# Four moves in the SP queue and half-size sums in the last unit of an attention and MLP kernel

## The chip, the cores and the metric

The program runs on one core of one Trainium2 chip. The time is the device time of one execution in microseconds (us). Before the change it is 294.99 us, the median of three runs (294.71 to 295.28).

## The reference

The inputs are q, k, v of 4 batches, 8 heads, 768 positions and 64 numbers each, a projection of 64 x 6, a gain of 512, and two weight matrices (512 x 2048 and 2048 x 512). Cut to what matters:

```python
q_bits = (q @ proj) > 0                          # six bits for each query, and for each key
k_bits = (k @ proj) > 0
mask   = (q_bucket[:, :, :, None] == k_bucket[:, :, None, :])   # all six bits agree
scores = np.where(mask, q @ k.T / 8, -1e9)
attn   = softmax(scores)
x      = (attn @ v), heads side by side          # 4 x 768 x 512
xn     = (x - mean) / sqrt(var + 1e-6) * g_ln    # over the 512
out    = x + np.maximum(xn @ w_ch1, 0) @ w_ch2
```

## The kernel before

**Work.** The 3072 rows of the output are cut into 12 units of 256 rows; unit u belongs to batch u // 3. A unit has two parts. In its attention, for each of two groups g of four heads and three pairs of key blocks (step s = 6u + 3g + kp), `S` multiplies bits and queries with keys into the PSUM tile `sc` (L570), `E` takes the exponential on ScalarE (L576), and `A` multiplies with v into `acc` (L595). `na` and `nb` divide by the row sums into the tile `x`, `nc` and `ag` make mean and variance, `rs` the inverse root on GpSimd (L635), and `ce` writes the centred rows `xc` in bf16 (L630), 128 rows at a time. In its MLP, `fl` turns `xc` into `xnT` with a DMA transpose, one for each 128 rows (L639). `F.u.p` is block p (256 of the 2048 hidden numbers) of the first layer (L659, eight matmuls), which needs both halves of `xnT`; `R.u.p` is its ReLU into `hb` (L667 on ScalarE, L669 on VectorE). The second layer of units 1 to 11 is a product of 2 x 2 blocks with seven products in place of eight: `P.u.k` is product k (L725, eight matmuls). Its left sides are quarters of `hb`, or the sums S1 to S4 of quarters that `ss.u.k` makes on VectorE (L710); S3 is written over a quarter of `hb`. `Y.u.k` adds what the product's PSUM tile holds to a quarter of `x` (L730). `O` stores finished rows (L742 and L744).

**PSUM.** The tiles of the tag `f` (first layer, products, bits) take two buffers in turns, by a list of digits in the kernel. Products 1, 6 and 7 add up in one tile X, products 5 and 3 in another, Yb, and in the last unit Ya (product 2), Yb and Yc (product 4) take the same buffer. So each `Y` has to read a tile before the next product adds to it or overwrites it.

**Loads.** `LX` loads 768 KB of q or k (L508), which `tu` turns on VectorE into `T` (L304) and `CA` casts. `hm` multiplies with the projection (L526), `bt` makes bits of it in the tile B, `mw` writes B to DRAM (L544), and four `mr` read it back, spread over the partitions, into G (L547, 24 KB each); `S` of that batch and group waits for all four. `lv` loads v (L467).

**Order.** All of it stands in one list of words, `ORDER`, written out as op.engine.arguments and issued one after the other; the engine letter is t (TensorE), v (VectorE), a (ScalarE), p (GpSimd) or s (the SP queue, which issues most DMAs). Each engine and the SP queue work through their own words in that order, so an instruction that waits holds up what stands behind it on its queue. The semaphores between the queues follow from the tiles that the instructions read and write.

Of the kernel before, what the change touches and what calls it, by code (L numbers as in the profile page):

```python
# [46 lines left out]
S.t.19.2 F.t.1.6 E.a.18.0 rs.p.2 F.t.1.3 CA.p.1.1.1 E.a.19.0 S.t.21.2 O.s.0.0 lv.s.1.4.1  # L47
E.a.19.1 A.t.19.2 E.a.21.0 R.v.1.6 sw.v.3.0 sw.v.2.0 E.a.21.1 F.t.1.0 R.a.1.0 lv.s.2.0.3
R.v.1.3 ce.v.2.1 sw.v.4.0 lv.s.1.4.0 ce.v.2.0 F.t.1.5 A.t.20.2 S.t.22.2 fl.s.2.1 tu.v.2.0.0.2
F.t.1.4 R.a.1.5 cv.p.1.4.0 A.t.18.2 LX.s.2.0.1 E.a.22.0 R.v.1.4 F.t.1.2 sp.t.1.0 sc.v.1.0  # L50
na.v.3.0 E.a.22.1 S.t.23.2 F.t.1.7 R.a.1.2 R.v.1.7 E.a.23.1 cv.v.1.4.2 E.a.23.0 F.t.1.1
sw.v.1.0 fl.s.2.0 R.a.1.1 nb.v.3.0 S.t.24.2 E.a.24.0 E.a.24.1 on.p.2 P.t.1.2 Y.v.1.2
F.t.2.1 R.a.2.1 su.p.1.4 S.t.26.2 lv.s.2.4.0 O.s.0.1 O.s.0.3 A.t.23.2 ss.v.1.1 P.t.1.1
P.t.1.5 ss.v.1.3 ss.v.1.2 tu.v.2.0.1.2 E.a.26.1 E.a.26.0 Y.v.1.1 lv.s.2.0.1 P.t.1.6 A.t.22.2
S.t.25.2 tu.v.2.0.0.3 ss.v.1.4 lv.s.2.4.3 E.a.25.0 Y.v.1.5 tu.v.2.0.0.0 Y.v.1.6 P.t.1.3 Y.v.1.3
# [13 lines left out]
F.t.3.7 R.a.3.7 F.t.3.0 tu.v.2.1.1.0 E.a.33.0 S.t.37.2 E.a.37.1 tu.v.2.1.1.1 E.a.37.0 tu.v.2.1.0.0  # L69
tu.v.2.1.1.3 tu.v.2.1.1.2 hm.t.2.1 O.s.2.0 CA.v.2.1.0 LX.s.3.0.0 bt.v.2.1 mw.s.2.1 mr.s.2.1.1 mr.s.2.1.3  # L70
S.t.38.2 F.t.3.5 R.v.3.0 A.t.34.2 R.a.3.5 F.t.3.3 CA.v.2.1.1 R.a.3.3 tu.v.3.0.1.0 E.a.38.1
A.t.35.2 F.t.3.4 A.t.33.2 O.s.2.2 nb.v.5.0 F.t.3.1 mr.s.2.1.2 R.a.3.4 na.v.5.1 tu.v.3.0.0.3
F.t.3.2 lv.s.3.4.1 E.a.38.0 R.a.3.1 rs.p.4 ce.v.4.1 S.t.36.2 P.t.3.2 R.a.3.2 E.a.36.1
nb.v.5.1 su.p.2.4 ss.v.3.1 Y.v.3.2 P.t.3.1 E.a.36.0 mr.s.2.1.0 S.t.39.2 E.a.39.1 E.a.39.0
O.s.2.3 ce.v.4.0 Y.v.3.1 nc.v.5.0 A.t.37.2 P.t.3.5 ss.v.3.2 ss.v.3.4 fl.s.4.1 LX.s.3.1.0
A.t.36.2 Y.v.3.5 cv.v.2.4.0 P.t.3.6 Y.v.3.6 P.t.3.3 A.t.38.2 ss.v.3.3 S.t.40.2 Y.v.3.3
E.a.40.0 E.a.40.1 P.t.3.7 nc.v.5.1 Y.v.3.7 tu.v.3.0.0.1 fl.s.4.0 F.t.4.3 ag.v.5.0 R.v.4.3
P.t.3.4 Y.v.3.4 O.s.3.1 O.s.3.0 S.t.41.2 E.a.41.1 E.a.41.0 sp.t.2.0 sc.v.2.0 F.t.4.0
ag.v.5.1 rs.p.5 F.t.4.4 R.a.4.4 na.v.6.0 R.v.4.0 O.s.3.3 ce.v.5.1 fl.s.5.1 S.t.44.2
E.a.44.1 tu.v.3.0.1.3 F.t.4.5 A.t.41.2 F.t.4.6 A.t.40.2 tu.v.3.0.0.2 E.a.44.0 R.a.4.6 tu.v.3.0.1.2  # L80
# [42 lines left out]
O.s.8.3 F.t.9.6 R.a.9.6 nb.v.11.0 ss.v.9.1 ss.v.9.2 S.t.70.2 E.a.70.1 A.t.71.2 ss.v.9.3  # L123
O.s.8.2 A.t.69.2 P.t.9.2 Y.v.9.2 ss.v.9.4 P.t.9.1 fl.s.10.0 E.a.70.0 Y.v.9.1 A.t.70.2
na.v.11.1 nb.v.11.1 fl.s.10.1 F.t.10.7 P.t.9.6 R.a.10.7 Y.v.9.6 nc.v.11.0 P.t.9.5 P.t.9.7
Y.v.9.5 Y.v.9.7 nc.v.11.1 P.t.9.3 Y.v.9.3 P.t.9.4 Y.v.9.4 O.s.9.3 O.s.9.0 O.s.9.2
F.t.10.6 R.a.10.6 ag.v.11.1 F.t.10.1 O.s.9.1 ag.v.11.0 rs.p.11 ce.v.11.0 fl.s.11.0 F.t.10.0
R.a.10.1 R.a.10.0 F.t.10.5 R.a.10.5 F.t.10.4 F.t.10.3 R.a.10.4 R.a.10.3 ce.v.11.1 fl.s.11.1
F.t.10.2 R.a.10.2 P.t.10.2 Y.v.10.2 F.t.11.4 R.a.11.4 ss.v.10.1 ss.v.10.2 P.t.10.1 Y.v.10.1
ss.v.10.4 P.t.10.5 Y.v.10.5 P.t.10.6 P.t.10.3 ss.v.10.3 Y.v.10.6 P.t.10.7 Y.v.10.3 F.t.11.0  # L130
R.a.11.0 Y.v.10.7 P.t.10.4 Y.v.10.4 O.s.10.2 F.t.11.2 R.a.11.2 F.t.11.5 R.a.11.5 F.t.11.7
F.t.11.1 R.a.11.7 R.a.11.1 F.t.11.6 F.t.11.3 R.a.11.6 P.t.11.2 R.a.11.3 ss.v.11.1 P.t.11.1
Y.v.11.2 ss.v.11.2 Y.v.11.1 ss.v.11.4 P.t.11.5 P.t.11.6 O.s.10.0 Y.v.11.5 P.t.11.3 ss.v.11.3
Y.v.11.6 P.t.11.7 O.s.10.1 Y.v.11.3 Y.v.11.7 O.s.10.3 O.a.11.0.1 O.s.11.0.0 Y.v.11.7.1.0 O.s.11.1.0.1
O.a.11.1.1.1 P.t.11.4 Y.v.11.4 O.a.11.1.1.0 O.s.11.1.0.0
"""


# [3 lines left out]
    E="012302132023132032103230103231032031230120302123031230120321013202120320",  # L142
# [10 lines left out]
    rs="012102102102",  # L153
# [12 lines left out]
def kernel(  # L166
# [15 lines left out]
    nc = tc.nc  # L182
    P = 128
    B, H, S, D = q.shape
# [11 lines left out]
    A = 4 * (D + 1)  # L196
# [34 lines left out]
    def sb(name, shape, dt, tag, bufs):  # L231
        if name not in made:
            if tag in SLOTS:
                n = taken.get(tag, 0)
                taken[tag] = n + 1
                tag, bufs = f"{tag}_{SLOTS[tag][n]}", 1
            made[name] = pool.tile(shape, dt, name=name, tag=tag, bufs=bufs)
        return made[name]
# [442 lines left out]
    def Hq(u, t, kh):  # L681
        return hb(u)[:, 8 * kh : 8 * kh + 8, P * t : P * t + P]
# [4 lines left out]
    def Ss(u, k):  # L687
        return Hq(u, 1, 0) if k == 3 else sb(f"S{u}{k}", [P, 8, P], BF16, "tp", 3)
# [9 lines left out]
        }[k]  # L698
        eng.tensor_tensor(out, in0, in1, op=op)

    def ss(eng, u, k):
        out, in0, in1, op = {
            1: (1, Hq(u, 1, 0), Hq(u, 1, 1), AOP.add),
            2: (2, None, Hq(u, 0, 0), AOP.subtract),
            3: (3, Hq(u, 0, 0), Hq(u, 1, 0), AOP.subtract),
            4: (4, Hq(u, 0, 1), None, AOP.subtract),
        }[k]
        in0 = Ss(u, 1) if in0 is None else in0
        in1 = Ss(u, 2) if in1 is None else in1
        eng.tensor_tensor(Ss(u, out), in0, in1, op=op)  # L710

    def prod(u, k):
        if k in (1, 6, 7) or (k == 4 and u < NU - 1):
# [21 lines left out]
    def O_(eng, u, *a):  # L735
# [13 lines left out]
        mem=mem, pmem=pmem, tab=tab, lp=lp, sel=sel, pf=pf, p32=p32c, warm=warm, wm=wm, lx=lx, tn=tn, ca=ca, ha=ha, bh=bh, hc=hc, bc=bc, sl=sl, bi=bi, lg=lg, gt=gt, gc=gc,  # L749
        lw1=lw1, wg=wg, lw2=lw2, on=on, lv=lv, cv=cv, su=su, sp=sp, sq=sq, sc=scp, LX=LX, gx=gx, tu=tu, CA=CA, hm=hm, bt=bt, mw=mw, mr=mr,  # L750
        S=S_, E=E_, A=A_, wa=wa, na=na, nb=nb, nc=nc_, ag=ag, ce=ce, rs=rs, fl=fl, ft=ft, fc=fc, F=F_, R=R_, D=D_, Z=Z_, P=P_, Y=Y_, sw=sw, ss=ss, O=O_,
    )
    ENGINES = dict(v=nc.vector, a=nc.scalar, p=nc.gpsimd, s=nc.sync, t=nc.tensor)
# [35 lines left out]
```

## Time and profile before

| | |
|---|---|
| median of three runs | 294.99 us (294.71 to 295.28) |
| profiled execution: its own time | 294.86 us |
| profiled execution: span of the instructions | 293.2 us |
| TensorE (PE) busy | 285.6 us, 97% of the span |
| VectorE (DVE), ScalarE (ACT), GpSimd (POOL) busy | 71%, 70%, 18% |
| TensorE clock granted | full in every slice |
| DMA moved | 34.10 MB, mean 116 GB/s |
| F, eight matmuls of 128x256 (L659) | 273 ns each, 94.2 us in all |
| ss, one sum of 128x1024 bf16 (L710) | 0.68 us |
| Y, one addition of 128x256 f32 (L730) | 0.42 us |
| fl, issue of one DMA transpose on the SP queue (L639) | 1.21 us |

A timeline row gives start, length, engine, line, operation and the number of instructions merged in it. Matmuls overlap: eight matmuls of 256 columns last 1.04 us from the start of the first to the end of the last, and the next eight begin 0.87 us after the first ones when nothing holds them up. The chain of waits goes back from the last instruction and names at each step what released it; its rows give start, length, and what ran.

### The profile page before, as it was taken

The numbers are of one execution on the slowest core, as the hardware profiler recorded it, in microseconds if no ns is written. First come the engines' busy times: TensorE is split into PE (matmuls) and PEld (weight loads), VectorE is DVE, ScalarE is ACT, GpSimd is POOL, SyncE is SP. The second block draws the span as 40 slices with busy tenths as digits, with TensorE's granted clock in tenths as the row PEclk, the third lists the DMA queues.
The fourth block names the chain that finished last, engine by engine and source line by source line (L and its number), as shares of the span: only waits on it lengthen the run. The fifth ranks groups of instructions, "written<-read, shape, count | busy, mean of one in ns | idle before, by whom it ended". The sixth has DMA issues, their size and how long they took to land.

```text
span 293.2 us, 10524 instructions
## 1 busy us (share of the span) xinstructions
PE 285.6 (97%) x4650; PEld 227.7 (78%) x4650; DVE 206.8 (71%) x474; ACT 206.2 (70%) x236; POOL 54.0 (18%) x88
## 2 busy tenths in 40 slices
PE   8999999999999999999999999999999999999994
PEld 4677778648788887878778778877888878897883
DVE  4757899996769795797667995866666654773433
ACT  4689999998966978784865896887793694515240
POOL 5261325222423005000300107210010010000000
PEclk9999999999999999999999999999999999999999
DMA  6999997747744692362330352230410402304022
GB/s 223 302 319 250 216 277 133 139 134 171 174 122 131 134 307 76 127 189 51 98 82 1 83 132 63 60 61 3 92 37 2 74 2 52 78 6 104 2 72 73
DMA packets 31055, 34.10 MB, mean 116 GB/s; under 512 B 15521, under 2 KB 27809, under 8 KB 31010
## 3 DMA queue, kind: packets, MB, share of 16 engines
q1 hardware_dynamic: 25938, 28.72, 35.6%
q0 software_dynamic: 4224, 4.19, 8.9%
q8 instruction: 36, 0.59, 0.9%
q10 hardware_dynamic: 848, 0.53, 0.7%
q14 instruction: 9, 0.07, 0.1%
HBM read 27.86 MB, written 6.88 MB: 118 GB/s over the span
## 4 chain that ended last, share of the span: by engine, by line
PE 91%; DMA 3%; DVE 2%; SPq 1%; ACT 1%; issue 0%; ACTq 0%; DVEq 0%
PE f L659 27%; PE sc L570 18%; PE X L725 13%; PE acc L595 12%; PE Yb L725 7%; PE hp L526 3%; PE Ya L725 3%; PE hf L394 3%; PE f L674 2%; PE warm L363 1%; ACT E L576 1%; DMA G<-Bd 1%; DMA Bd<-B 1%; PE warm L366 1%; DMA xnT<-xc 1%; SPq L547 1%
## 5 line engine op out<-in xcount | busy, mean ns | idle before, releaser
L576 ACT ACTIVATE E<-sc,bias_sb 128x1024 bf16<-128x1024 f32 x144 | 153.1, 1111 | 36.0 <-PE sc L570 32.6
L659 PE MATMUL f<-xnT,w_sb 128*128 128x256 bf16 x768 | 94.2, 273 | 0.7 <-DMA xnT<-xc 0.6
L659 PEld LDWEIGHTS <-w_sb 128*128 128x128 bf16 x768 | 71.4, 98 | 13.6 <-issue 5.7
L667 ACT ACTIVATE hb<-f 128x512 bf16<-128x512 f32 x67 | 39.6, 598 | 34.5 <-PE f L659 34.5
L570 PE MATMUL sc<-qb,kb 32*128 32x256 bf16 x1152 | 52.5, 267 | 0.0
L595 PEld LDWEIGHTS <-E 128*128 128x128 bf16 x1152 | 40.8, 98 | 4.0 <-issue 2.5
L595 PE MATMUL acc<-vaug,E 128*128 128x65 bf16 x1152 | 43.7, 194 | 0.1
L570 PE MATMUL sc<-G 6*128 6x256 bf16 (+1 forms) x576 | 42.7, 273 | 1.1 <-ACT E L576 0.8
L725 PEld LDWEIGHTS <-hb 128*128 128x128 bf16 x352 | 33.4, 98 | 5.4 <-issue 1.3
L570 PEld LDWEIGHTS <-kb 32*128 32x128 bf16 x1152 | 30.5, 93 | 1.5
L635 POOL TENSOR_SCALAR rs<-mv 128x2 f32<-128x2 f32 x12 | 3.3, 277 | 150.4 <-DVE mv L624 150.4
L730 DVE TENSOR_TENSOR x<-X,x 128x256 f32<-128x256 f32 x44 | 18.4, 419 | 16.5 <-PE X L725 16.3
L570 PEld LDWEIGHTS <-G 6*128 6x128 bf16 (+1 forms) x576 | 16.0, 91 | 16.7 <-issue 13.3
L725 PEld LDWEIGHTS <-S 128*128 128x128 bf16 x264 | 25.0, 98 | 4.8 <-issue 1.4
L669 DVE TENSOR_SCALAR hb<-f 128x512 bf16<-128x512 f32 x29 | 19.7, 681 | 12.0 <-PE f L659 11.8
L304 DVE STREAM_TRANSPOSE T<-X 128x384 f32<-128x384 f32 (+2 forms) x52 | 26.1, 535 | 0.0
L725 PE MATMUL Yb<-w_sb,S 128*128 128x256 bf16 x176 | 22.9, 273 | 0.0
L608 DVE SCALAR_TENSOR_TENSOR y<-vsB,acc 128x520 f32<-128x520 f32 x24 | 16.5, 689 | 8.1 <-PE acc L595 7.8
L725 PE MATMUL X<-wt,hb 128*128 128x256 bf16 x168 | 21.8, 273 | 0.0
L617 DVE TENSOR_TENSOR x<-y,rc 128x512 f32<-128x512 f32 x24 | 17.8, 742 | 0.8
L621 DVE BATCH_NORM_STATS2 st<-x 128x6 f32<-128x256 f32 x48 | 17.4, 412 | 0.2
L730 DVE TENSOR_TENSOR x<-Yb,x 128x256 f32<-128x256 f32 x22 | 9.2, 420 | 9.5 <-PE Yb L725 9.5
(95 smaller groups left out, 268.3 us busy)
## 6 DMA issues: line engine op xcount, KB each, us to landing
out_dram<-x SPq DMA_DIRECT2D x45, 128.0 KB
X<-in_k_dram SPq DMA_DIRECT2D x7, 768.0 KB
vn<-in_v_dram SPq DMA_DIRECT2D x24, 192.0 KB
X<-in_q_dram SPq DMA_DIRECT2D x6, 768.0 KB
w_sb<-in_moe_w_ch_dram POOLq DMA_DIRECT2D x8, 512.0 KB, 10.8
vn<-in_v_dram SPq DMA_DIRECT2D x2, 768.0 KB
X<-in_q_dram SPq DMA_DIRECT2D x2, 512.0 KB
Bd<-B SPq DMA_DIRECT2D x6, 96.0 KB
```

The lines of the kernel that those rows point to most:

```text
L304: nc.vector.transpose(d[:, j], s[:, j, kj0 : kj0 + n])
L570: nc.tensor.matmul(sc(s, i // 2)[:, i % 2, 256 * kk : 256 * kk + 256], lh, rh, start=(rep == 0), stop=(rep == 2), skip_group_check=True,)
L576: nc.scalar.activation(E(s)[:, heads(h)], sc(s, h), AF.Exp, scale=EXP_SCALE, bias=bias_sb)
L595: nc.tensor.matmul(acc[:, qt, (D + 1) * i : (D + 1) * (i + 1)], E(s)[:, i, 256 * kk + P * qt : 256 * kk + P * qt + P], vaug(u // 3)[:, 4 * ...
L608: nc.vector.scalar_tensor_tensor(yt(u, g), vs, EPS_ROW, made[f"acc{u}{g}"][:, :, :A], op0=AOP.mult, op1=AOP.add,)
L617: nc.vector.tensor_tensor(xo, a[:, :, :, 0:D], rc.to_broadcast([P, 2, 4, D]), op=AOP.mult)
L621: nc.vector.bn_stats(stats(u)[:, qt, g], xt(u)[:, qt, 256 * g : 256 * g + 256])
L659: nc.tensor.matmul(f1[:, n].rearrange("p (t x) -> p t x", t=2), w1_sb[:, dt, P * nt : P * nt + P], xnT(u)[:, :, dt], start=(dt == 0), stop ...
L667: nc.scalar.activation(hb(u)[:, 2 * p : 2 * p + 2], f1, AF.Relu)
L669: eng.tensor_scalar_max(hb(u)[:, 2 * p : 2 * p + 2], f1, 0.0)
L725: nc.tensor.matmul(f2, lh[:, n], rh[:, n], start=(first and n == 0), stop=(n == 7), skip_group_check=True)
L730: nc.vector.tensor_tensor(x, made[f"{prod(u, k)}{u}"], x, op=AOP.add)
```

## The change

Four groups of words are moved on the SP queue, and the last unit is written otherwise:

1. `LX.s.2.0.1` (768 KB of k) goes behind `fl.s.2.0`; before, it stood between the two transposes of unit 2.
2. The last two reads of bits, `mr.s.2.1.2` and `mr.s.2.1.0`, go ahead of the store `O.s.2.2` and the load `lv.s.3.4.1`, right behind the first two.
3. `LX.s.3.1.0` (768 KB of q) goes behind `fl.s.4.0`; before, it stood between the two transposes of unit 4.
4. The four stores of unit 9 go behind both transposes of unit 11. (Three stores of unit 10 also stand earlier in the list, but in the same place among SP's words.)
5. The first layer of unit 11 takes its blocks in the order 4 0 5 1 7 2 6 3, not 4 0 2 5 7 1 6 3. Each of its four sums is two instructions of 128x512: the first halves of all four stand after `R.a.11.1`, the second halves where the whole sums stood (after the last ReLU, between the Y).

Cut to its core (reflowed lines of the list are left out):

```diff
-F.t.1.4 R.a.1.5 cv.p.1.4.0 A.t.18.2 LX.s.2.0.1 E.a.22.0 R.v.1.4 F.t.1.2 sp.t.1.0 sc.v.1.0
...
-sw.v.1.0 fl.s.2.0 R.a.1.1 nb.v.3.0 S.t.24.2 E.a.24.0 E.a.24.1 on.p.2 P.t.1.2 Y.v.1.2
...
+fl.s.2.0 LX.s.2.0.1 R.a.1.1 nb.v.3.0 S.t.24.2 E.a.24.0 E.a.24.1 on.p.2 P.t.1.2 Y.v.1.2
...
-A.t.35.2 F.t.3.4 A.t.33.2 O.s.2.2 nb.v.5.0 F.t.3.1 mr.s.2.1.2 R.a.3.4 na.v.5.1 tu.v.3.0.0.3
+A.t.35.2 F.t.3.4 A.t.33.2 mr.s.2.1.2 mr.s.2.1.0 O.s.2.2 nb.v.5.0 F.t.3.1 R.a.3.4 na.v.5.1
...
-O.s.2.3 ce.v.4.0 Y.v.3.1 nc.v.5.0 A.t.37.2 P.t.3.5 ss.v.3.2 ss.v.3.4 fl.s.4.1 LX.s.3.1.0
...
+E.a.40.1 P.t.3.7 nc.v.5.1 Y.v.3.7 tu.v.3.0.0.1 fl.s.4.0 LX.s.3.1.0 F.t.4.3 ag.v.5.0 R.v.4.3
...
-Y.v.9.5 Y.v.9.7 nc.v.11.1 P.t.9.3 Y.v.9.3 P.t.9.4 Y.v.9.4 O.s.9.3 O.s.9.0 O.s.9.2
-F.t.10.6 R.a.10.6 ag.v.11.1 F.t.10.1 O.s.9.1 ag.v.11.0 rs.p.11 ce.v.11.0 fl.s.11.0 F.t.10.0
...
+F.t.10.4 F.t.10.3 R.a.10.4 R.a.10.3 ce.v.11.1 fl.s.11.1 O.s.9.3 O.s.9.0 O.s.9.2 O.s.9.1
...
-R.a.11.0 Y.v.10.7 P.t.10.4 Y.v.10.4 O.s.10.2 F.t.11.2 R.a.11.2 F.t.11.5 R.a.11.5 F.t.11.7
-F.t.11.1 R.a.11.7 R.a.11.1 F.t.11.6 F.t.11.3 R.a.11.6 P.t.11.2 R.a.11.3 ss.v.11.1 P.t.11.1
...
+R.a.11.0 Y.v.10.7 P.t.10.4 Y.v.10.4 O.s.10.2 F.t.11.5 R.a.11.5 F.t.11.1 R.a.11.1 ss.v.11.1.0
+ss.v.11.2.0 ss.v.11.3.0 ss.v.11.4.0 F.t.11.7 F.t.11.2 R.a.11.7 R.a.11.2 F.t.11.6 F.t.11.3 R.a.11.6
+R.a.11.3 P.t.11.2 ss.v.11.1.1 P.t.11.1 Y.v.11.2 O.s.10.0 O.s.10.1 O.s.10.3 P.t.11.5 ss.v.11.2.1
+Y.v.11.1 P.t.11.6 ss.v.11.4.1 Y.v.11.5 P.t.11.3 ss.v.11.3.1 Y.v.11.6 P.t.11.7 Y.v.11.3 Y.v.11.7
...
-    def ss(eng, u, k):
+    def ss(eng, u, k, *part):
+        r = slice(4 * part[0], 4 * part[0] + 4) if part else slice(0, 8)
...
-        eng.tensor_tensor(Ss(u, out), in0, in1, op=op)
+        eng.tensor_tensor(Ss(u, out)[:, r], in0[:, r], in1[:, r], op=op)
```

More of the change, by code (lines that the diff above doesn't have):

```diff
@@ L49 @@
 R.v.1.3 ce.v.2.1 sw.v.4.0 lv.s.1.4.0 ce.v.2.0 F.t.1.5 A.t.20.2 S.t.22.2 fl.s.2.1 tu.v.2.0.0.2
-F.t.1.4 R.a.1.5 cv.p.1.4.0 A.t.18.2 LX.s.2.0.1 E.a.22.0 R.v.1.4 F.t.1.2 sp.t.1.0 sc.v.1.0
-na.v.3.0 E.a.22.1 S.t.23.2 F.t.1.7 R.a.1.2 R.v.1.7 E.a.23.1 cv.v.1.4.2 E.a.23.0 F.t.1.1
-sw.v.1.0 fl.s.2.0 R.a.1.1 nb.v.3.0 S.t.24.2 E.a.24.0 E.a.24.1 on.p.2 P.t.1.2 Y.v.1.2
+F.t.1.4 R.a.1.5 cv.p.1.4.0 A.t.18.2 E.a.22.0 R.v.1.4 F.t.1.2 sp.t.1.0 sc.v.1.0 na.v.3.0
+E.a.22.1 S.t.23.2 F.t.1.7 R.a.1.2 R.v.1.7 E.a.23.1 cv.v.1.4.2 E.a.23.0 F.t.1.1 sw.v.1.0
+fl.s.2.0 LX.s.2.0.1 R.a.1.1 nb.v.3.0 S.t.24.2 E.a.24.0 E.a.24.1 on.p.2 P.t.1.2 Y.v.1.2
 F.t.2.1 R.a.2.1 su.p.1.4 S.t.26.2 lv.s.2.4.0 O.s.0.1 O.s.0.3 A.t.23.2 ss.v.1.1 P.t.1.1
@@ L71 @@
 S.t.38.2 F.t.3.5 R.v.3.0 A.t.34.2 R.a.3.5 F.t.3.3 CA.v.2.1.1 R.a.3.3 tu.v.3.0.1.0 E.a.38.1
-A.t.35.2 F.t.3.4 A.t.33.2 O.s.2.2 nb.v.5.0 F.t.3.1 mr.s.2.1.2 R.a.3.4 na.v.5.1 tu.v.3.0.0.3
-F.t.3.2 lv.s.3.4.1 E.a.38.0 R.a.3.1 rs.p.4 ce.v.4.1 S.t.36.2 P.t.3.2 R.a.3.2 E.a.36.1
-nb.v.5.1 su.p.2.4 ss.v.3.1 Y.v.3.2 P.t.3.1 E.a.36.0 mr.s.2.1.0 S.t.39.2 E.a.39.1 E.a.39.0
-O.s.2.3 ce.v.4.0 Y.v.3.1 nc.v.5.0 A.t.37.2 P.t.3.5 ss.v.3.2 ss.v.3.4 fl.s.4.1 LX.s.3.1.0
-A.t.36.2 Y.v.3.5 cv.v.2.4.0 P.t.3.6 Y.v.3.6 P.t.3.3 A.t.38.2 ss.v.3.3 S.t.40.2 Y.v.3.3
-E.a.40.0 E.a.40.1 P.t.3.7 nc.v.5.1 Y.v.3.7 tu.v.3.0.0.1 fl.s.4.0 F.t.4.3 ag.v.5.0 R.v.4.3
+A.t.35.2 F.t.3.4 A.t.33.2 mr.s.2.1.2 mr.s.2.1.0 O.s.2.2 nb.v.5.0 F.t.3.1 R.a.3.4 na.v.5.1
+tu.v.3.0.0.3 F.t.3.2 lv.s.3.4.1 E.a.38.0 R.a.3.1 rs.p.4 ce.v.4.1 S.t.36.2 P.t.3.2 R.a.3.2
+E.a.36.1 nb.v.5.1 su.p.2.4 ss.v.3.1 Y.v.3.2 P.t.3.1 E.a.36.0 S.t.39.2 E.a.39.1 E.a.39.0
+O.s.2.3 ce.v.4.0 Y.v.3.1 nc.v.5.0 A.t.37.2 P.t.3.5 ss.v.3.2 ss.v.3.4 fl.s.4.1 A.t.36.2
+Y.v.3.5 cv.v.2.4.0 P.t.3.6 Y.v.3.6 P.t.3.3 A.t.38.2 ss.v.3.3 S.t.40.2 Y.v.3.3 E.a.40.0
+E.a.40.1 P.t.3.7 nc.v.5.1 Y.v.3.7 tu.v.3.0.0.1 fl.s.4.0 LX.s.3.1.0 F.t.4.3 ag.v.5.0 R.v.4.3
 P.t.3.4 Y.v.3.4 O.s.3.1 O.s.3.0 S.t.41.2 E.a.41.1 E.a.41.0 sp.t.2.0 sc.v.2.0 F.t.4.0
@@ L125 @@
 na.v.11.1 nb.v.11.1 fl.s.10.1 F.t.10.7 P.t.9.6 R.a.10.7 Y.v.9.6 nc.v.11.0 P.t.9.5 P.t.9.7
-Y.v.9.5 Y.v.9.7 nc.v.11.1 P.t.9.3 Y.v.9.3 P.t.9.4 Y.v.9.4 O.s.9.3 O.s.9.0 O.s.9.2
-F.t.10.6 R.a.10.6 ag.v.11.1 F.t.10.1 O.s.9.1 ag.v.11.0 rs.p.11 ce.v.11.0 fl.s.11.0 F.t.10.0
-R.a.10.1 R.a.10.0 F.t.10.5 R.a.10.5 F.t.10.4 F.t.10.3 R.a.10.4 R.a.10.3 ce.v.11.1 fl.s.11.1
+Y.v.9.5 Y.v.9.7 nc.v.11.1 P.t.9.3 Y.v.9.3 P.t.9.4 Y.v.9.4 F.t.10.6 R.a.10.6 ag.v.11.1
+F.t.10.1 ag.v.11.0 rs.p.11 ce.v.11.0 fl.s.11.0 F.t.10.0 R.a.10.1 R.a.10.0 F.t.10.5 R.a.10.5
+F.t.10.4 F.t.10.3 R.a.10.4 R.a.10.3 ce.v.11.1 fl.s.11.1 O.s.9.3 O.s.9.0 O.s.9.2 O.s.9.1
 F.t.10.2 R.a.10.2 P.t.10.2 Y.v.10.2 F.t.11.4 R.a.11.4 ss.v.10.1 ss.v.10.2 P.t.10.1 Y.v.10.1
 ss.v.10.4 P.t.10.5 Y.v.10.5 P.t.10.6 P.t.10.3 ss.v.10.3 Y.v.10.6 P.t.10.7 Y.v.10.3 F.t.11.0
-R.a.11.0 Y.v.10.7 P.t.10.4 Y.v.10.4 O.s.10.2 F.t.11.2 R.a.11.2 F.t.11.5 R.a.11.5 F.t.11.7
-F.t.11.1 R.a.11.7 R.a.11.1 F.t.11.6 F.t.11.3 R.a.11.6 P.t.11.2 R.a.11.3 ss.v.11.1 P.t.11.1
-Y.v.11.2 ss.v.11.2 Y.v.11.1 ss.v.11.4 P.t.11.5 P.t.11.6 O.s.10.0 Y.v.11.5 P.t.11.3 ss.v.11.3
-Y.v.11.6 P.t.11.7 O.s.10.1 Y.v.11.3 Y.v.11.7 O.s.10.3 O.a.11.0.1 O.s.11.0.0 Y.v.11.7.1.0 O.s.11.1.0.1
-O.a.11.1.1.1 P.t.11.4 Y.v.11.4 O.a.11.1.1.0 O.s.11.1.0.0
+R.a.11.0 Y.v.10.7 P.t.10.4 Y.v.10.4 O.s.10.2 F.t.11.5 R.a.11.5 F.t.11.1 R.a.11.1 ss.v.11.1.0
+ss.v.11.2.0 ss.v.11.3.0 ss.v.11.4.0 F.t.11.7 F.t.11.2 R.a.11.7 R.a.11.2 F.t.11.6 F.t.11.3 R.a.11.6
+R.a.11.3 P.t.11.2 ss.v.11.1.1 P.t.11.1 Y.v.11.2 O.s.10.0 O.s.10.1 O.s.10.3 P.t.11.5 ss.v.11.2.1
+Y.v.11.1 P.t.11.6 ss.v.11.4.1 Y.v.11.5 P.t.11.3 ss.v.11.3.1 Y.v.11.6 P.t.11.7 Y.v.11.3 Y.v.11.7
+O.a.11.0.1 O.s.11.0.0 Y.v.11.7.1.0 O.s.11.1.0.1 O.a.11.1.1.1 P.t.11.4 Y.v.11.4 O.a.11.1.1.0 O.s.11.1.0.0
 """
```

## The prediction

> **What bounds the kernel now.** The page first: who is busy, and who is on the chain that ended last.
>
> ```profile
> PE 285.6 (97%) x4650; PEld 227.7 (78%) x4650; DVE 206.8 (71%) x474; ACT 206.2 (70%) x236; POOL 54.0 (18%) x88
> PE 91%; DMA 3%; DVE 2%; SPq 1%; ACT 1%; issue 0%; ACTq 0%; DVEq 0%
> ```
>
> TensorE is the bound; it does the same matmuls after the change, at a clock granted in full. So a gain can only come from its pauses, and these are few. The timeline of PE marks two behind its first 31 us, both released by a DMA; two more don't show as idle and are found by spacing. Eight matmuls of 256 columns take 1.04 us, and the next eight begin 0.87 us after the first unless held.
>
> The first is in the chain around 78 us:
>
> ```profile
> 77.78 0.98 PE Ya L725 x8
> 78.76 1.03 PE f L659 x8
> ```
>
> The timeline has the starts at 77.72 and 78.75: 1.03 apart, so PE ran empty for 0.16. The second row is `F.2.1`, the first to read unit 2's `xnT`. By the completion marks in the trace, `fl.2.0`, issued at 71.79, landed at 78.70, right after the 768 KB of `LX.2.0.1` (issued at 71.11, landed at 77.50). A transpose with little ahead of it lands in 2.5 us.
>
> The second is in the chain around 128 us:
>
> ```profile
> 122.38 0.68 SPq L547
> 123.05 0.05 issue
> 123.11 0.66 SPq L547
> 123.77 0.05 issue
> 123.82 0.43 SPq L744
> ...
> 124.30 0.67 SPq L547
> ...
> 125.08 0.37 SPq L467
> ...
> 125.50 3.16 DMA G<-Bd
> 128.66 0.05 issue
> 128.70 0.84 PE sc L570 x23
> ```
>
> The four reads of bits (L547) are broken up by a store (L744) and a load (L467); the last lands at 128.66 and `S.39` starts then. The product ahead of it started at 127.36; from a product to an `S` it is 0.97 elsewhere (136.20 to 137.17), so 128.33 was possible: 0.37 lost.
>
> The third is in the chain around 267 us:
>
> ```profile
> 267.39 2.48 DMA xnT<-xc
> 269.87 0.14 issue
> 270.01 1.03 PE f L659 x8
> ```
>
> `F.11.4` waits for `fl.11.1`. `P.10.2` began at 268.37, so 269.24 was possible: 0.77 lost. `fl.11.1` was late because SP first issued four stores (262.91 to 265.98) and only then the two transposes (266.09 and 267.39), while VectorE had both halves of `xc` ready at 265.20.
>
> The fourth is the last unit's products, by VectorE's and PE's timelines:
>
> ```profile
> 283.69 0.42 DVE L730 TENSOR_TENSOR x<-Ya,x 128x256 f32<-128x256 f32 x1
> 284.63 0.42 DVE L730 TENSOR_TENSOR x<-X,x 128x256 f32<-128x256 f32 x1
> ```
>
> ```profile
> 284.17 1.03 PE L725 MATMUL Yb<-w_sb,S 128*128 128x256 bf16 x8
> 285.10 1.03 PE L725 MATMUL X<-wt,S 128*128 128x256 bf16 x8
> ```
>
> `Y.11.2` ends at 284.11 and `P.11.5`, which takes its buffer, starts at 284.17; `Y.11.1` ends at 285.05 and `P.11.6`, which adds to its tile, starts at 285.10. The next two pairs do the same (285.98 and 286.03, 286.91 and 286.96). VectorE alternates whole sums (0.68) and Y (0.42), 0.93 a pair; PE would go at 0.87 but follows.
>
> **The change, part by part.**
>
> *`LX.2.0.1` behind `fl.2.0`.* `xc` is ready at 70.85, SP free at 71.06: `fl.2.0` goes at 71.11 and by the row of `fl.2.1` (issued 69.86, landed 72.70, 2.84) lands near 74, far ahead of 78.59. Gain **0.16** (bounds 0 and 0.16). The load goes at 72.4, 1.2 later, and with its 6.4 us lands near 78.8. Its first reader, a transpose on VectorE, ran at 81.07: 2.1 us of cover.
>
> *The reads of bits.* Back to back they go at 122.38, 123.11, 123.8 and 124.5; the three not behind a load land 2.23 after issue (124.30 to 126.53), so the last lands near 126.8, 1.5 before 128.33. Gain **0.37** (bounds 0 and 0.37). The store and `lv.3.4.1`, put behind them, go up to 1.4 us later; SP reaches `fl.4.1` at the same time, and nobody needs the two soon. At nothing.
>
> *`LX.3.1.0` behind `fl.4.0`.* Before, `fl.4.0` landed at 134.96 and `F.4.3`, its reader, ran at 135.32: no pause yet. But the two gains above bring `F.4.3` to 134.79, and 0.17 would come back. With `fl.4.0` at about 128.4 it lands near 131. So this move gains nothing and keeps 0.17 (counted above). The load lands some 2 us later, near 135; `tu` needs it after 145.
>
> *The stores of unit 9 behind the transposes of unit 11.* SP now meets `fl.11.0` first. It waits for `xc` (264.74); behind it wait the second transpose and the eight stores of units 9 and 10, and nobody needs a store before the end. `fl.11.0` goes at 264.8, `fl.11.1` 1.25 later at 266.05, landed by 2.48 at 268.53: 0.7 before 269.24. What is late next? Unit 10's products move up by 0.77, but its sums on VectorE only as far as ScalarE's ReLU allows, which was done at 269.17. I stepped through the row lengths: S1 269.79, S2 270.50, `Y.10.1` 271.18, S4 271.53, `Y.10.5` 272.12, S3 272.46, `Y.10.6` 273.06 to 273.48. `P.10.7`, the tightest, may start at 273.62 and needs the last 0.05 after its end: free by 0.09. Gain **0.77** (bounds 0.5, if VectorE sets the pace there as in the last unit, four times 0.06, and 0.77). The stores go near 267.3 to 269; no reader.
>
> *Halves in the last unit.* The last two blocks of the first layer stay 6 and 3, so the last ReLU still ends at 283.05. The first halves need blocks 0, 1, 4 and 5 only; `R.11.1`, now the fourth ReLU, ends near 279.5, and VectorE idles for 5.44 us up to 283.08. Four halves hide there even at 0.68 each. Behind the last ReLU a half stands where a sum stood. No row shows a bf16 sum of 128x512. Bounds: half of 0.68 is 0.34, and the top is 0.68 unchanged. Nearest is the Y row, 256 four-byte columns, the same bytes: 0.42. I take 0.42. Then the half of S1 runs 283.08 to 283.50, `Y.11.2` 283.43 to 283.85, and `P.11.5` starts at PE's own 284.00. VectorE needs 0.69 a pair where PE needs 0.87, so PE sets the pace: starts at 284.00, 284.87, 285.75, 286.62, and `P.11.4` at 287.49, not 287.83. Gain **0.34** (bounds 0, for 0.68, and 0.34; up to 0.50 nothing is lost). What follows `P.11.4` (its Y, the last stores) is unchanged.
>
> The Trainium skill speaks against halving: "VectorE: DVE Perf Modes", section on the TRN2 errata, has a fixed cost for every instruction, so many small ones pay it many times. With its measured fixed term of about 150 cycles and two bf16 elements a cycle, my estimate from that page is 0.42 for a half, against 0.34 by halving the row; by either the gain is 0.34, as the four extra fixed costs fall into idle time.
>
> **Sum.** 0.16 + 0.37 + 0.77 + 0.34 = 1.64. The profiled execution took 294.86 (span 293.2), so 293.22; the median is 0.13 above the profiled one: **293.4** (293.35).
>
> **Rivals.**
>
> 1. *Part of it is given back.* PE moves up by 0.5 behind 128 us, and a wait with less cover than that (an exponential on ScalarE, a late `xnT`, VectorE in unit 10) takes its place. For: ScalarE is 70% busy, and the 0.09 in unit 10 is thin. Against: between 32 and 267 us the chain is PE but for the stretch of the bits, and ScalarE itself waits for PE 32.6 us in `E`. Without the third term's lower third and one of the small ones, 0.5 to 1.1 is left: 293.9 to 294.5.
> 2. *It doesn't do what it says.* The late transfers are late for another reason than what was issued ahead (the transposes wait for DMA engines still busy with `lv` loads, which land up to 72.23; the reads are slow by themselves), and a half costs as much as a whole. Then nothing moves: 295.0. Against: the same transfers are fast wherever no load is ahead.
> 3. *Slower: the 768 KB for unit 2 come too late.* The place is VectorE's transpose at 81.07 (80.9 with the gain); `Y.1.1` is behind it, and the second half of unit 1's products behind that. VectorE has 0.43 idle before `Y.1.1`; each us past 81.3 then costs one. The slowest load of this size landed 8.3 after issue (101.71 to 109.97): 80.7, just in time. It decides against the change from 11.2 us on, landing at 83.6: 293.4 + 2.3 = 295.7. Against: only the order of issues changed, not the bytes, and all were in by 78.70.
>
> **Numbers.** About 0.2% (0.6 us) is what a measurement of this kernel can tell from no change. Forecast 0.72; rival 1 0.17 (mostly still faster by over 0.2%); rival 2 0.06; rival 3 0.05. The range runs from 293.0 (the forecast, less the spread of runs, 0.3) to 294.2, which leaves out rivals 2 and 3 and the worse part of rival 1. Faster 0.87, within 0.2% 0.08, slower 0.05.
>
> **What would show it.** In the new profile: `F.2.1` 0.87 behind the product ahead of it; four L547 rows in a row near 122 and no idle before `S.39`; `fl.11.0` issued ahead of the stores and no wait at `F.11.4`; the last unit's products 0.87 apart, with halves of about 0.42. No pause marked on PE behind 31 us. A pause of PE at 82 to 86 us (rival 3), at 134 to 136, or products of unit 10 at 0.93, would make the prediction wrong.

## The result: 293.04 us, and the profile after

The changed kernel takes 293.04 us (median of 9 runs, 292.02 to 295.29), the kernel before 295.05 us in the same comparison; the ratio is 0.9932, with a 95% interval of 0.9903 to 0.9961. Forecast were 293.4 us and a range of 293.0 to 294.2. The profiled execution took 293.44 us, with a span of 291.7 us against 293.2. (The profiled executions of four experiments, `stores`, `reads`, `shift` and `poolstores`, ran at half the clock for 3 to 10 us between 30 and 57 us, so of these only distances further on are read, and no time; the other ten are called full-clock below.)

The page of the profile after, engines and chain. DMA and the SP queue are gone from the chain:

```profile
PE 284.7 (98%) x4648; PEld 227.9 (78%) x4650; DVE 207.4 (71%) x478; ACT 206.2 (71%) x236; POOL 54.0 (19%) x88
PE 95%; DVE 2%; ACT 1%; issue 0%; ACTq 0%; DVEq 0%
```

The chain of waits of the profile after, around 78, 128 and 268 us: what follows now follows at PE's own pace (0.87 us for eight matmuls of 256 columns; 0.98 behind an `S`).

```profile
78.02 0.98 PE Ya L726 x8
79.00 0.87 PE f L659 x8
...
127.61 0.87 PE X L726 x8
128.48 0.77 PE sc L570 x24
...
268.25 0.87 PE Ya L726 x8
269.12 0.87 PE f L659 x8
```

The SP queue's timeline of the profile after (start, length, line, operation, count): both transposes of unit 2 and then the load; four reads in one row; the transposes of unit 11 and then the stores.

```profile
70.10 2.52 SPq L639 DMA_TRANSPOSE xnT<-xc  x2
72.67 0.57 SPq L508 DMA_DIRECT2D X<-in_k_dram  x1
...
123.57 2.80 SPq L547 DMA_DIRECT2D G<-Bd  x4
...
264.53 2.50 SPq L639 DMA_TRANSPOSE xnT<-xc  x2
267.08 1.97 SPq L745 DMA_DIRECT2D out_dram<-x  x4
```

VectorE and PE in the last unit of the profile after, from their timelines: halves of 0.41 to 0.43, and products 0.87 apart.

```profile
279.00 0.43 DVE L711 TENSOR_TENSOR S<-S,hb 128x512 bf16<-128x512 bf16 x1
...
282.71 0.41 DVE L711 TENSOR_TENSOR S<-S,hb 128x512 bf16<-128x512 bf16 x1
```

```profile
282.95 1.04 PE L726 MATMUL Yb<-w_sb,S 128*128 128x256 bf16 x8
283.82 1.04 PE L726 MATMUL X<-wt,S 128*128 128x256 bf16 x8
```

Laying the starts of the same matmuls in the two traces side by side gives the account. After minus before steps by -0.15 us at `F.2.1`, -0.38 at `S.39`, -0.76 at `F.11.4` and -0.35 over the last unit's products, 1.64 in all; +0.25 came in between 44 and 59 us, where nothing was changed. The last products start 1.39 us earlier, and the span is 1.42 us shorter (1.5 by the rounded figures above).

### The profile page after: what moved, and what is told of

Its sections match the earlier page's. It is cut to its first block, busy times and chain, and to the rows that moved or that the text cites. A ratio compares the mean times of both kernels' runs of the same rounds, so it can differ in the third digit from the quotient of the medians.

```text
span 291.7 us, 10527 instructions
## 1 busy us (share of the span) xinstructions
PE 284.7 (98%) x4648; PEld 227.9 (78%) x4650; DVE 207.4 (71%) x478; ACT 206.2 (71%) x236; POOL 54.0 (19%) x88
## 4 chain that ended last, share of the span: by engine, by line
PE 95%; DVE 2%; ACT 1%; issue 0%; ACTq 0%; DVEq 0%
PE f L659 30%; PE sc L570 18%; PE X L726 13%; PE acc L595 12%; PE Yb L726 7%; PE Ya L726 3%; PE hp L526 3%; PE hf L394 3%; PE f L674 2%; PE warm L363 1%; ACT E L576 1%; PE warm L366 1%; DVE xnT L652 0%; PE hf L405 0%; PE vp L487 0%
```

## The experiments

The theory: the change takes four pauses out of PE's path, worth what the profiled execution showed. The rivals in question: the pauses are not the same in every execution, so the four figures are one draw; a pause has another cause than the order of SP's words; only part of an edit does the work.

Below, a pause is the distance of two starts less 0.87 us (less 0.97 for an `S` behind a product), worked out from each trace; "unit 11" is the four distances from `P.11.1` to `P.11.7` less four times 0.87. The experiments' files number lines otherwise: a store is L711, a transpose L605, a product L692, an ss L677, an `F` L625, an `S` L536, a `Y` L697, a read of bits L513, a load of v L433 (in `shift` a store is L746 and a transpose L641).

| kernel: parts made | F.2.1 | S.39 | F.4.3 | F.11.4 | unit 11 |
|---|---|---|---|---|---|
| before: none | 0.16 | 0.37 | 0.02 | 0.77 | 0.35 |
| before_again: none | 0.01 | 1.58 | 0.01 | 0.23 | 0.34 |
| before_third: none | 0.01 | 0.02 | 0.10 | 0.47 | 0.35 |
| blocks: block order of 5 | 0.01 | 1.51 | 0.01 | 0.43 | 0.35 |
| halves: halves of 5 | 0.01 | 0 | 0.01 | 0.49 | 0 |
| sums: 5 | 0.01 | 0.07 | 0.42 | 0 | 0 |
| early: 1, 2, 3 | 0.01 | 0 | 0.01 | 0.68 | 0.35 |
| reads: 2 | 0.01 | 0 | 0.27 | 1.07 | 0.34 |
| stores: 4 | 0.13 | 0.90 | 0.01 | 0 | 0.35 |
| no3: 1, 2, 4, 5 | 0.01 | 0 | 0.71 | 0 | 0 |
| shift: none, code moved | 0.01 | 0.51 | 0.01 | 0 | 0.35 |
| poolstores: none, stores of unit 9 on GpSimd | 0.01 | 0.86 | 0.01 | 0.79 | 0.35 |
| after, all_again: all | 0.01 | 0 | 0.01 | 0 | 0 |

**all_again: the change once more.**

```diff
 (no edit: the changed kernel)
```

> The change as it is, once more, with a second profile. Theory (four pauses of PE taken out, 0.16 + 0.37 + 0.77 + 0.34 = 1.64 us): the four places show matmul groups 0.87 us apart again, and the time is 1.6 us below before, about 293.4. Rival (the measured 2.0 us holds a gain that the four places do not show): 293.0 or less, and PE starts of this profile run ahead of those of before by more than 1.64 us at the end, with a step at a fifth place.

292.82 us (10 runs, 292.03 to 294.61), ratio 0.9945 (0.9918 to 0.9972). No pause at any of the five places. Its last matmul starts 2.18 us ahead of that of before: 1.64 at the four places, and 0.55 in the first seven us, where this execution's warm-up matmuls came to full pace earlier. So there is a fifth step, as the rival says, but in the start, which the change does not touch.

**stores, sums, early: one group of parts each.**

```diff
 stores
-Y.v.9.4 O.s.9.3 O.s.9.0 O.s.9.2 F.t.10.6 R.a.10.6 ag.v.11.1 F.t.10.1 O.s.9.1 ... fl.s.11.1
+Y.v.9.4 F.t.10.6 R.a.10.6 ag.v.11.1 F.t.10.1 ... fl.s.11.1 O.s.9.3 O.s.9.0 O.s.9.2 O.s.9.1
 sums: everything from O.s.10.2 on as in the change
 early
-fl.s.2.1 LX.s.2.0.1 ... fl.s.2.0 ... mr.s.2.1.3 ... O.s.2.2 ... mr.s.2.1.2 ... mr.s.2.1.0 ... fl.s.4.1 LX.s.3.1.0 ... fl.s.4.0
+fl.s.2.1 fl.s.2.0 LX.s.2.0.1 ... mr.s.2.1.3 ... mr.s.2.1.2 mr.s.2.1.0 O.s.2.2 ... fl.s.4.1 ... fl.s.4.0 LX.s.3.1.0
```

> Part 4 alone: the four stores of unit 9 behind both transposes of unit 11, all else as before. Theory: F.11.4 starts 0.87 us behind P.10.2, a step of 0.77 us in PE's starts there and none elsewhere; 294.3 us against 295.05. Rival (given back by VectorE's sums in unit 10): the products of unit 10 follow each other at 0.93 us, step 0.77 and then back to 0.5; 294.5 us.

> Part 5 alone: the last unit's block order and half sums, all else as before. Theory: the products of unit 11 start 0.87 us apart, PE's last start is 0.34 us earlier; 294.7 us. Rival (a half costs as much as a whole, or P waits for the half itself): products at 0.93 us as before, no step; 295.0 us.

> Parts 1, 2 and 3 alone: the three moves around 71 and 122 to 130 us, all else as before. Theory: steps of 0.16 us at F.2.1 and 0.37 us at S.39 and no pause at F.4.3; the wait at F.11.4 stays; 294.5 us. Rival (the part of the gain that the sum did not forecast sits here, since the bits' way through DRAM varies from run to run and before had no cover for it): more than 0.53 us, 294.1 or less.

Ratios: stores 0.9964 (0.9928 to 0.9999), sums 0.9982 (0.9954 to 1.001), early 0.9951 (0.9925 to 0.9976); in us of 295, 1.1, 0.5 and 1.4, each give or take 0.8 to 1.0. They add up to 3.0, more than the 2.0 and 1.6 of the whole change, which intervals this wide allow; that of `sums` takes in no gain at all. In each, the pauses of its own parts are gone and the products of unit 10 go at 0.87 to 0.90 us, so nothing is given back there. But `early` gained more than 0.53, as its rival had it, and in `sums`, where parts 1 to 4 are not made, the pauses at `F.2.1` and `F.11.4` were away all the same and one of 0.42 stood at `F.4.3`. The pauses are not constants; the next runs ask what sets them.

**before_again and before_third: the order of before, profiled twice more.**

```diff
-    def ss(eng, u, k):
+    def ss(eng, u, k, *part):
 (as in the change, but the list of words is that of before, so that no sum is halved)
```

> The order of before, once more, for a second profile of it (the sums' function takes an optional part that is not used). Theory (the pauses of the profiled execution are not the same in every execution): F.2.1, S.39, F.4.3 and F.11.4 are held by 0 to 1 us each, not by 0.16, 0.37, 0.02 and 0.77 again; the pace of the last unit's products, which depends on no transfer, is 0.93 us again. Rival (they are fixed): the same four figures within 0.05.

> The order of before, a third profile. Theory: the pauses at F.2.1, S.39, F.4.3 and F.11.4 differ again from both profiles so far; S.39 is held longest where the code transfer near 122 us meets the write of the bits to DRAM (landing 3.7 us after issue rather than 2.6), and F.11.4 where the one near 264 us meets the four stores. Their sum with the 0.35 us of the last unit is 0.8 to 2.2 us. Rival: one of the two profiles repeats within 0.05 us at each place.

The five pauses add up to 1.67, 2.17 and 0.95 us in the three profiles of before, 1.60 in the mean. Only unit 11's, which hangs on no transfer, repeats. The largest is `S.39` in `before_again`; its chain of waits:

```profile
123.84 0.66 SPq L513
...
124.55 0.43 SPq L711
...
125.81 0.38 SPq L433
...
126.23 3.11 DMA G<-Bd
...
129.39 0.84 PE sc L536 x24
```

The same store and load stand among the reads as before, but all of it begins 0.73 later (123.11 against 122.38), since the write of the bits, issued at 119.20, landed only 3.85 us later. Of the ten traces at full clock, four have the write in after 1.9 to 2.6 us (before, before_third, sums, halves: pauses of 0 to 0.37), six after 3.4 to 3.9 (before_again and blocks: 1.58 and 1.51; early, no3, after and all_again, with part 2: none). I had expected the transfer of 16 KB near 122 us on the queue that the page calls "q8 instruction" (a code transfer, below) to make the difference. It doesn't: in all ten it begins 2.7 to 3.3 us after the issue of the write, with a pause or without. What goes with the write is `LX.3.0.0`, the load of 768 KB issued 2.7 us ahead of it on the same queue: by the completion marks the write lands 0.29 to 0.33 us after the last part of that load in all ten, and the load takes 4.3 to 6.3 us.

What makes its last part late can be narrowed down from the same traces. The load leaves sixteen completion marks. In all fourteen traces fifteen of them are in by 4.4 us after its issue; the last comes at 4.2 to 6.3. In thirteen a code transfer begins between 0.40 us before the load's issue and 0.12 after it. Where it took 0.95 to 1.11 us (five traces) the last mark came at 4.3 to 5.0, where it took 1.22 to 1.67 (eight) at 5.7 to 6.3, and in `shift`, the one trace without a code transfer there, at 4.2. (In `shift` one began 1.2 us after the issue of the write, and the write landed 1.7 us after the load.) So in the ten it is the code transfer near 116 us, not the one near 122, that goes with the late write. That it is the cause is not shown: no run was made for it, and moving that load was not tried. Nor is a late write the only way to a pause here: in `poolstores` the write was in after 2.0 us, but the second read, with a code transfer beginning 0.03 us after its issue, took 1.75 us to issue instead of 0.66, and `S.39` was held by 0.86.

**reads: part 2 alone.**

```diff
-mr.s.2.1.3 ... O.s.2.2 ... mr.s.2.1.2 ... mr.s.2.1.0
+mr.s.2.1.3 ... mr.s.2.1.2 mr.s.2.1.0 O.s.2.2
```

> Part 2 alone: the four reads of bits back to back, the two loads of 768 KB between their transposes. Theory: S.39 is not held (0.97 us behind P.3.1), and F.4.3, which comes forward by what S.39 lost before, is held by 0.1 to 0.7 us, since fl.4.0 still lands behind LX.3.1.0. Rival (the reads are late by themselves, by the write ahead of them): S.39 is held by 0.1 us or more.

The write is late here too (3.64 us), and `S.39` is not held; the rival, that the reads are late by themselves, falls: part 2 gives cover for a late write as well, here and in the four full-clock profiles that have it. `F.4.3` is held by 0.27, as expected without part 3.

**shift: the code transfers moved.**

```diff
+        for _ in range(64):
+            nc.tensor.matmul(wp[:, 0, :64], ones, ones[:, :64], start=True, stop=True)
```

> The order of before, with 64 more warm-up matmuls of 64 columns in front (they add work, some 4 to 7 us, and no data). They put 128 more instructions ahead of PE's program, so a 16 KB code transfer (queue 8, 0.9 to 1.6 us long) meets other places in it: 64 pairs are some 7 us of first-layer blocks, so the one at 264.0 falls near 257 and the next, at 279.5 before, near 272. Theory (the wait at F.11.4 came from the code transfer that met the four stores): the fourth store's issue takes 0.4 us, not 1.7, fl.11.1 lands in time, and F.11.4 is held by less than 0.1 us, though the stores stand ahead of the transposes. Rival (the stores alone delay the transposes): held by 0.5 us or more.

The 128 instructions more (64 matmuls with their weight loads) made 37 transfers of 16 KB on queue 8, where every other trace has 36, and moved them along PE's program; that is why they are called code transfers here. The answer on DMA for 264.0 to 265.5 us of before, with queue 8: its share of 16 engines, 6.6% of 1.5 us, is 1.58 us of one engine.

```profile
q1 hardware_dynamic: 118, 0.30, 73.3%
q8 instruction: 1, 0.02, 6.6%
```

In that stretch the fourth store of unit 9 took 1.77 us to issue, and `before_again` (1.23), `early` (1.69) and `blocks` (1.43) show the same; in these four the code transfer begins 0.9 to 1.3 us after the issue of the first store. In `before_third` and `halves` it begins 1.7 us after it and strikes one place later: all four stores issue in 0.3 to 0.4 each, and `fl.11.0` takes 2.2 us. In `sums` it begins 2.0 us after it; `fl.11.0` takes 1.48 and `F.11.4` is not held, so a meeting need not hold PE up. In `shift` no code transfer falls between the stores and the transposes, and the SP timeline is clean with the stores still ahead:

```profile
271.44 1.72 SPq L746 DMA_DIRECT2D out_dram<-x  x4
273.34 2.50 SPq L641 DMA_TRANSPOSE xnT<-xc  x2
```

`F.11.4` is not held (0). So in this profile the stores alone cost nothing; in every profile in which the place was held, a code transfer met the stores or the transposes. The reverse, a code transfer without stores, shows in the same traces at `fl.7.1`, where no store is near: in before one begins at 196.43, 0.56 us after the issue, and in `shift` there is none (the first line is of before, the second of `shift`):

```profile
195.87 1.99 SPq L639 DMA_TRANSPOSE xnT<-xc  x1
...
204.39 1.20 SPq L641 DMA_TRANSPOSE xnT<-xc  x1
```

In all fourteen traces together, behind 40 us, a code transfer began within 0.72 us after the issue of a transpose 31 times, and each of these took 1.48 to 2.70 us to issue; the 250 whose issue no code transfer overlapped took 1.19 to 1.38. At `fl.6.1` and `fl.7.1`, 25 of the 31, no more than 2 KB of other data moved meanwhile. So a code transfer by itself lengthens a transpose's issue if it begins in that stretch. One that begins shortly before the issue did as much only with other transfers under way: 0.22 and 0.23 us before `fl.11.0`, with the stores running, 2.2 us (`before_third`, `halves`); 0.24 us before it, without stores, 1.19 (`stores`). Part 4 takes the stores out of the meeting. In the four profiles that have it the code transfer begins 0.24 to 0.97 us before `fl.11.0`; what one just after the issue would cost there was not met.

**poolstores: the stores on another queue.**

```diff
-Y.v.9.4 O.s.9.3 O.s.9.0 O.s.9.2 ... O.s.9.1 ag.v.11.0 rs.p.11
+Y.v.9.4 ... ag.v.11.0 rs.p.11 O.p.9.3 O.p.9.0 O.p.9.2 O.p.9.1
```

> The order of before, but the four stores of unit 9 go out on GpSimd's queue, right behind rs.11, so that their data move at the time of the transposes and SP does not issue them. Theory (what held the transposes is SP's queue): fl.11.0 is issued when xc is ready, near 264.8 on before's scale, and F.11.4 is not held. Rival (the stores' traffic delays the transposes, whoever issues them): fl.11.0 is issued early too, but its data land 1 us or more later than the usual 2.5, and F.11.4 is held by 0.3 us or more.

SP was free and issued both transposes at once, the first at 270.65, yet they landed 4.4 and 3.8 us later instead of 2.4. The chain of waits:

```profile
271.96 3.78 DMA xnT<-xc
275.73 0.14 issue
275.87 1.03 PE f L625 x8
```

`F.11.4` is held by 0.79. The stores (issued from 269.95 to 272.14) and a code transfer at 270.46 ran beside it. So the rival holds: it is the traffic and not only the queue that issues it; stores on this queue without a code transfer were not met. In this one profile the stores on another queue did the same harm; behind the transposes they did none in the four profiles with part 4.

**no3: without part 3.**

```diff
-fl.s.4.1 ... fl.s.4.0 LX.s.3.1.0
+fl.s.4.1 LX.s.3.1.0 ... fl.s.4.0
```

> The change without its part 3: LX.3.1.0 stands between the transposes of unit 4 again. Theory: F.4.3 is held by 0.1 to 0.5 us, since fl.4.0 lands behind the load near 134 to 135 and the moves ahead of it bring F.4.3 forward; the other pauses stay away. Rival (the part is of no use): F.4.3 0.88 us behind the product ahead of it.

```profile
133.18 0.99 PE X L692 x8
...
134.19 0.43 DVE x L697
...
134.69 1.03 PE f L625 x8
```

The chain names VectorE's Y of product 7, the one that ended last. But `F.4.3` does not use that tile; `fl.4.0` landed at 134.55 by the trace's completion marks, 0.14 ahead of the start, the same 0.14 as in the chains at `F.11.4`. Held by 0.71, more than the 0.1 to 0.5 expected: part 3 does more than keep 0.17. `reads` shows it too (0.27), and `sums` (0.42), where an early start had brought PE forward.

**halves and blocks: part 5 in two.**

```diff
 halves: order 4 0 2 5 7 1 6 3 kept
-R.a.11.7 R.a.11.1 F.t.11.6 ... R.a.11.3 ss.v.11.1 P.t.11.1 Y.v.11.2 ss.v.11.2
+R.a.11.7 R.a.11.1 ss.v.11.1.0 ss.v.11.2.0 ss.v.11.3.0 ss.v.11.4.0 F.t.11.6 ... R.a.11.3 ss.v.11.1.1 P.t.11.1 Y.v.11.2 ss.v.11.2.1
 blocks: as the change from O.s.10.2 on, with whole sums where the second halves stand
```

> The order of before, with the last unit's sums in halves but its blocks in the old order 4 0 2 5 7 1 6 3; the first halves stand after R.11.1, which is then the sixth ReLU. Theory (only what VectorE has to do behind the last ReLU counts): the first halves run in about 1.6 us between the sixth ReLU (281.3 on before's scale) and the last (283.05), and the products of unit 11 start 0.87 us apart. Rival (the block order is needed to get the first halves out of the way): the last of them runs into the last ReLU, and P.11.5 is 0.95 us or more behind P.11.1.

> The order of before, with the last unit's blocks in the new order 4 0 5 1 7 2 6 3 and its four sums whole. Theory (the block order alone does nothing): products of unit 11 at 1.04, 0.93, 0.93 and 0.93 us as before. Rival: nearer to 0.87.

PE's timeline of `halves`, then of `blocks`: 0.87 and 0.88 apart, against 1.03 and 0.94.

```profile
281.51 1.04 PE L692 MATMUL X<-w_sb,hb 128*128 128x256 bf16 x8
282.38 1.04 PE L692 MATMUL Yb<-w_sb,S 128*128 128x256 bf16 x8
283.26 1.04 PE L692 MATMUL X<-wt,S 128*128 128x256 bf16 x8
```

```profile
282.96 1.04 PE L692 MATMUL X<-w_sb,hb 128*128 128x256 bf16 x8
283.99 1.03 PE L692 MATMUL Yb<-w_sb,S 128*128 128x256 bf16 x8
284.93 1.03 PE L692 MATMUL X<-wt,S 128*128 128x256 bf16 x8
```

In `halves` the first halves run from 279.72 to 281.28 and the last ReLU releases the next at 281.47: just in time without the new block order. The halving does all of it; the block order adds cover only. None of the versions tried has fewer pauses than the change.

## Why the prediction was right

- *The fourth term, 0.34* (the last unit): 0.35 wherever it was measured. The half costs 0.41 to 0.43, the value taken from the Y row and not the half of 0.68. The estimate of 0.42 worked out from the Trainium skill, "VectorE: DVE Perf Modes", section on the TRN2 errata, agrees with it. As reckoned, the four extra fixed costs lie in idle time (278.54 to 280.10).
- *The third, 0.77*: 0.76 between the two profiles, and unit 10's sums held nothing up, as stepped through. But 0.77 was near the top of what the place costs: the full-clock profiles without part 4 show 0 to 0.77 (before, before_again, before_third, blocks, halves, sums, early: mean 0.44); only `reads`, at 1.07, and `poolstores`, at 0.79, show more. The step "`fl.11.1` was late because SP first issued four stores" was half the cause: in `shift` the same order costs nothing. A code transfer had to meet the stores or the transposes; the fourth store's 1.77 us of issue, four times its neighbours' 0.42, stood in the profile and was not asked about.
- *The second, 0.37*: 0.38 between the two profiles, but 0 to 1.58 in the six full-clock profiles without part 2, 0.59 in the mean. It was sized too small, by as much as the third was too large. What was not asked was when the write ahead of the reads lands, which hangs on the last part of the load ahead of it. In the profile after it landed 3.7 us after issue, and the last read at 128.00, 0.4 us ahead of its need and not 1.5. The forecast of no pause held, but with a quarter of the cover it had reckoned.
- *The first, 0.16*: 0.15 between the two profiles, 0.01 in five further full-clock profiles without part 1. There `fl.2.0` landed 5.6 to 6.2 us after issue in the same order, not 6.9. Part 1 was not tried by itself.
- *Part 3*, "gains nothing and keeps 0.17": undone in one profile, it costs 0.71.
- *The sum*: 1.64 forecast, 2.0 and 1.6 measured (intervals of 1.2 to 2.9 and 0.8 to 2.4 us), 1.60 as the mean of three profiles of before. The way in which each pause goes was right, but the agreement of the sum is in good part luck: the pauses of one profile were taken for the kernel's, and the errors of size cancelled. Of the two medians, 293.04 lies just inside the range and 292.82 just below it.
- *Rivals*: none came. The load of part 1 landed at 77.22, sooner than the 78.8 reckoned, well ahead of its reader; no pause stands at 82 to 86 us.
- *Landings reckoned too early*: the transposes put ahead of a load did not land near 74 and 131 but at 75.52 and 133.15, 4.1 and 3.9 us after issue, not 2.8 and 2.5. A code transfer began 1.9 and 1.0 us after their issue; that it was the cause is not shown. It did no harm: `F.2.1` started 3.3 us later, `F.4.3` 1.9.

## What to carry to other kernels

A pause that ends with a DMA is one draw: profile the kernel before two or three times, and compare transfers of a kind (issue time, time to landing) before you price it. Moving what is not urgent behind what PE waits for gains the mean pause; here it left none in any profile that had the move (five for the reads, four for the stores), whether the transfers were late or not. When an issue or a landing is slow for its kind, look at what else the DMA engines carry at that moment, the code included. Where an engine alternates two kinds of work and sets another's pace, ask which part of its work has its data already; that part can run earlier, even if it costs more in all.

## What was not expected of the hardware

- Code comes by DMA in 16 KB pieces (36 packets of queue 8 in a run, 37 in `shift`), each a single packet, most of them 0.9 to 1.7 us long, and other transfers feel it. Behind 40 us, 95 of the 1774 DMA issues on SP in the fourteen traces took over 0.3 us more than the median of their kind (0.4 for a store, 1.2 for a transpose), and a code transfer overlapped each of the 95. With a code transfer beside it and the stores of unit 9 under way, a transpose landed 3.4 to 4.4 us after issue instead of 2.4 (`before_third`, `halves`, `sums`, `poolstores`). `shift` moved the code transfers, and the slow issues moved with them.
- A small transfer behind a large one on the same queue lands with it: the 96 KB write of bits 0.3 us after the 768 KB load in all ten full-clock traces, and `fl.4.0` 0.5 to 2.1 us after `LX.3.1.0` where it stands behind it.
- The start varies by itself. The matmuls begin at half pace, those of 512 columns 0.43 us apart. The first of those that follow at 0.22 starts at 4.0 to 6.9 us in the ten full-clock traces, 2.9 to 5.8 us after the first matmul. This moves all that follows: the first `S` starts between 8.09 (`halves`) and 8.95 (`early`), 0.86 apart, which is more than any of the four terms. The Trainium skill, "TensorE: Matmul & The Clock Gate", Part 1, puts the change of pace around 4 us into sustained matmuls, give or take 0.5 us; the traces agree on the middle (4.3 us in the mean of the ten) and show a wider spread.
